# Attention and two feed-forward layers on one core: a transposed block is put in with the next pair's first blocks, and two weight chunks' low parts change engine

## The chip, the cores and the metric

The kernel runs on 1 core of one Trainium2 chip. The metric is the device time of one execution in microseconds (us). The engines are named as the profile names them: PE (TensorE; its weight loads are PEld), DVE (VectorE), ACT (ScalarE), POOL (GpSimd), SP (SyncE, which issues nearly all DMAs here). A difference below 0.2% (2 us) counts as no change.

## The reference

```python
# q, k, v: (4, 8, 576, 64), f: (4, 8, 576)
scores = matmul(q, k.T) / sqrt(64)
cum    = cumsum(log(clip(f, 1e-4, 1)))
scores = where(causal, -1e9, scores + cum[:, None] - cum[None, :])
attn   = softmax(scores)                    # over the keys
x = matmul(attn, v)                         # to (2304, 512)
h = x @ w_in0;  x = (h - tanh(h)) @ w_out0  # 512 -> 2048 -> 512
h = x @ w_in1;  x = (h * sigmoid(h)) @ w_out1
```

## The kernel before

Everything is float32. A product is made of three or four passes over high and low parts, so that PE does the most of the work. The program has two stages: the attention, which takes the first 178 us or so and in whose last part the first layer already begins, and the two feed-forward layers, which the change does not touch.

**The attention.** The 32 heads are worked off as 16 pairs p (`NP`). A pair has 576 queries: four blocks of 128 for each head and a last block of 64, and the last 64 queries of both heads share one tile of 128 rows. So a pair has nine tiles, grouped into four units u: unit 0 holds the query blocks 0 and 1 of both heads, unit 1 block 2, unit 2 block 3, and unit 3 the shared tile of the last queries. For each tile DVE adds the mask to the scores and takes the row's extreme (`least`, L462), ACT takes the exponential (`expo`, L470), POOL multiplies with one over the row's sum (`normalise`, L484). PE then transposes the tile block by block (`transposes`, L495) into the PSUM tiles `t`, each 2 KiB wide and four blocks of 128 columns long; ACT and DVE copy them to `ptf` in SBUF (`evac`, L535), and PE multiplies them with the values (`values`, L546). There are three buffers for the tiles `t` and two for the score tiles `s` (`scores`, L449 and, for the last queries, L441).

**The order of the work** is written out by hand under `manual_schedule`: a table `due` names for each of some 150 steps (a step is a tile; nine to a pair) what is called, and each engine runs its instructions in that order. The transposes of unit 3 of pair p come at the same place as the transposes of units 0, 1 and 2 of pair p+1 a few steps later (`steps_`, L620). Within a step the order is: transposes, values and scores on PE; then the copies (`evac`), the exponential, the extreme, the normalising, the loads and splits of a later pair (L385 on DVE, L383 and L391 on POOL), and last the decoding of weights.

**A round**, in what follows, is the time from PE's transposes of one pair's last queries (L495, source `pt`, five of them) to those of the next. On PE a round holds: unit 3 of pair p, unit 0 of pair p+1, the scores of unit 2 of pair p+2 (L449, 64x512), the transposes of unit 1, the scores of the last queries of pair p+2 (L441), the transposes of unit 2, the values of pair p, and the scores of units 0 and 1 of pair p+3. The scores of the last queries take the PSUM buffer of the scores of unit 1, so PE may begin them only when DVE has done `least` for both tiles of unit 1 (128x384 each).

**The fifth block.** The last queries have 576 keys, four and a half blocks of 128, so there are five transposes. Four go into one tile `t`, the fifth into column block 0 of a second one. That second tile is kept in `spare`; the next pair's unit 0 puts its two blocks of query block 0 ("the first blocks") into column blocks 1 and 2 of it. DVE copies the fifth block (128x128) and ACT the first blocks (128x256).

**Weights.** The two layers' weights come as 64-bit numbers and are decoded to a high and a low part, in 32 chunks of two matrices (m = 0, 1), each in seven stages (`wstages`, L143 on): `scale` (L153) and `split` (L163) on ACT; `shift` (L157), `exponent` (L167) and `low` (L170) on DVE; `rest` (L176) and `join` (L180) on POOL for chunks 0 to 4 and on DVE for the others. Chunks 0 and 1 are decoded during the attention, a stage every three to four steps (L657); chunks 2 to 4 at its end.

Of the kernel before, what the change touches and what calls it, by code (L numbers as in the profile page):

```python
# [7 lines left out]
F32 = mybir.dt.float32  # L8
# [6 lines left out]
P = 128  # L15
# [17 lines left out]
NEARLY, MID, LATE = 2, 3, 6  # L33
# [6 lines left out]
def forgetting_attention_two_ffn(  # L40
# [12 lines left out]
    nc = tc.nc  # L53
# [9 lines left out]
    def rd(ap):  # L63
        return ap.bitcast(F32)
# [78 lines left out]
    def wstages(k):  # L143

        l, c = chunks[k]
        slot = k % NSLOT
        tag = {m: f"{l}_{c}_{m}" for m in range(2)}
        a, b, w = {}, {}, {}
        eng = nc.gpsimd if k < NEARLY + MID else nc.vector

        def scale(m):
            high = rd(raws[k, m][:, :, 1])
            nc.scalar.activation(high, high, AF.Prelu, scale=2.0 ** -112, alpha=-(2.0 ** 32))  # L153

        def shift(m):
            a[m] = wtmp.tile([P, DM], U32, tag="wa", name=f"wa{tag[m]}")
            nc.vector.tensor_scalar(a[m], raws[k, m][:, :, 1], 3, None, ALU.logical_shift_left)  # L157

        def split(m):
            hi, lo = w[m] = [  # L160
                wpool[slot].tile([P, DM], F32R, tag=f"w{s}{slot}_{m}", name=f"w{s}{tag[m]}") for s in "hl"
            ]
            nc.scalar.copy(hi, rd(a[m]))  # L163

        def exponent(m):
            b[m] = wtmp.tile([P, DM], F32, tag="wb", name=f"wb{tag[m]}")
            nc.vector.tensor_scalar(b[m].bitcast(U32), a[m], 0xFF800000, None, ALU.bitwise_and)  # L167

        def low(m):
            nc.vector.scalar_tensor_tensor(  # L170
                b[m], raws.pop((k, m))[:, :, 0], 2.0 ** -52, b[m], ALU.mult, ALU.mult
            )

        def rest(m):
            hi, lo = w[m]
            eng.tensor_tensor(lo, rd(a[m]), rd(hi), ALU.subtract)  # L176

        def join(m):
            hi, lo = w[m]
            eng.tensor_tensor(lo, rd(lo), b[m], ALU.add)  # L180
            wtiles[l, c, m] = (hi, lo)

        return [(fn, m) for fn in (scale, shift, split, exponent, low, rest, join) for m in range(2)]
# [4 lines left out]
    def wdecode(k, left=0):  # L188


        if k not in stages:
            stages[k] = wstages(k)
        while len(stages[k]) > left:
            fn, m = stages[k].pop(0)
            fn(m)
            if not stages[k] and k > 1:
                wload(k + 2)
# [129 lines left out]
    def attention():  # L327
        with ExitStack() as actx:
# [4 lines left out]
            def pool(stack, name, bufs=1, **kw):  # L333
                return stack.enter_context(tc.tile_pool(name=name, bufs=bufs, side="right", **kw))
# [7 lines left out]
            ps_t = pool(actx, "ps_t", 3, space=PSUM)  # L342
# [4 lines left out]
            NP = B * NPAIR  # L347
# [5 lines left out]
            pt4 = [sp.tile([P, 640], F32, name=f"pt4_{i}", bufs=1) for i in range(2)]  # L353

            out_t = ps_r.tile([P, 512], F32, name="out_t")
            out_0, spare = {}, {}

            ptfs = [ptp.tile([P, 2, NPT], F32, name=f"ptf{i}") for i in range(2)]

# [63 lines left out]
            sps, ptile, rowsum, tps = {}, {}, {}, {}  # L423
# [62 lines left out]
            def transposes(p, u):  # L486

                ptf = ptfs[p % 2]
                rest = spare.pop("t", None) if u == 0 else spare.clear()
                tp = [ps_t.tile([P, 4, P], F32, tag="t", name=f"t{p}_{u}_{j}") for j in range(1 if rest else 2)]  # L490
                if rest:
                    tp.append(rest[:, 1:])

                def turn(j, k, pt, c):
                    nc.tensor.transpose(tp[j][:, k], pt[:, c * P:c * P + P], ident)  # L495

                def place(j, c0, nc_, i):
                    n = 2 * nc_
                    q = P * i + 448 * c0
                    dst = ptf[:, :, q:q + 448 * nc_] if nc_ > 1 else ptf[:, :, q:q + P]  # L500
                    src = tp[j][:, 0:n]
                    if nc_ > 1:
                        dst = dst.rearrange("p h (c w) -> p h c w", w=448)[:, :, :, 0:P]
                        src = src.rearrange("p (h c) w -> p h c w", h=2)
                    return src, dst

                if u == 3:
                    ptile.pop((p, 2, 4))
                    pt = pt4[p % 2]
                    spare["t"] = tp[1]  # L510
                    for c in range(5):
                        turn(c // 4, c % 4, pt, c)
                    dst = ptf[:, :, 512:512 + 4 * 448].rearrange("p h (c w) -> p c h w", w=448)[:, :, :, 0:64]
                    o = 448 * 4 + 512
                    tps[p, u] = [
                        (tp[0].rearrange("p c (h w) -> p c h w", h=2), dst),
                        (tp[1][:, 0].rearrange("p (h w) -> p h w", h=2), ptf[:, :, o:o + 64]),
                    ]
                    return
                pts = {t: ptile.pop((p,) + t)[0] for t in units[u]}  # L520
                i = u + 1
                if u == 0:
                    for h in range(2):
                        turn(1, h, pts[h, 0], 0)
                for j in range(2 if u else 1):
                    for h in range(2):
                        for k in range(min(2, i + 1 - 2 * j)):
                            turn(j, min(2, i + 1 - 2 * j) * h + k, pts[h, i], 2 * j + k)
                tps[p, u] = [place(j, 2 * j, min(2, i + 1 - 2 * j), i) for j in range(2 if u else 1)]
                if u == 0:  # L530
                    tps[p, u].append(place(1, 0, 1, 0))

            def evac(p, u):
                for j, (src, dst) in enumerate(tps.pop((p, u))):
                    (nc.vector.tensor_copy if j == (u > 0) else nc.scalar.copy)(dst, src)  # L535

            def values(p, part):

# [83 lines left out]
            for p in range(NP):  # L622
                n0 = NTILE * p
                for u, k in enumerate((-1, 0, 4, 6)):
                    if p + u:
                        later(n0 + k, scores, p, u)
                k = ends_.get(p, steps_)
                for u in range(4):
                    later(n0 + k[u], transposes, p, u)
                    later(n0 + k[u] + 1, evac, p, u)  # L630
                later(n0 + k[4], values, p, [(0, 0), (64, 0), (64, 1), (64, 2), (64, 3), (64, 4)])
                later(n0 + k[4] + 1, collect, p, 0, 64)
                later(n0 + k[4] + 1, collect, p, 64, S)
# [35 lines left out]
            for n in range(N + 2 * NTILE):  # L669
                if n % NTILE == 0:  # L670
                    run(n, scores)
                    run(n, transposes)
                    run(n, values)
                else:
                    run(n, transposes)
                    run(n, values)
                    run(n, scores)
                if n < NTILE - 1:
                    busy(kqs[0][:, 0], 2)
                run(n, evac)  # L680
                if has(n - 1):
                    expo(n - 1)
                run(n, collect)
                if n % 3 == 2 and has(n - 5):
                    guard(n - 5)
                if has(n):
                    least(tiles[n])
                if n % 3 == 2 and has(n - 5):
                    normalise(n - 5)
                run(n, load_kq, load_v, split, place_last, place_dec, place_dec_last)  # L690
                for fn, *a in ahead.get(n - N, []):
                    fn(*a)
# [4 lines left out]
    with tc.manual_schedule():  # L697
        attention()
        for n in range(len(steps) + HL):
            if n > HL:  # L700
                front(n)
            if n >= HL:
                project(n - HL)
# [39 lines left out]
```

## Time and profile before

| what | value |
|---|---|
| median of 3 runs | 984.08 us (983.68 to 984.15) |
| the profiled execution's own time | 984.0 us |
| its span, first to last instruction | 982.1 us |
| PE busy | 964.6 us, 98% of the span |
| DVE, ACT, POOL busy | 555.8, 454.8, 183.6 us |
| granted clock of PE | 1.0 throughout |

How to read it: a share of busy time is a mean over the whole program. POOL works only in the first 210 us and is busy there nearly all the time; DVE and ACT are busy some seven tenths of the attention. In a timeline a row gives the start, the duration, engine, line, operation, the tiles written and read, the shape, how many instructions are put together, and in brackets the idle time ahead of the first of them with what ended it. Matmuls overlap, so the duration of several is less than their sum.

### The profile page before, as it was taken

How to read it: one execution, taken by the hardware profiler on the slowest of the kernel's cores; microseconds unless marked ns; L12 is line 12 of the kernel's file. 1: busy time of each engine (PE TensorE's matmuls, PEld its weight loads, DVE VectorE, ACT ScalarE, POOL GpSimd, SP SyncE). 2: the span in 40 equal slices, each digit the busy share in tenths (PEclk: the TensorE clock that was granted, in tenths of full speed). 3: DMA queues.
4: the chain of work that ended last, by engine and by line, in shares of the span. 5: the costliest groups of instructions: out<-in, count | busy, mean ns of one | idle time of the engine just before them, and what ended most of it. 6: DMA issues, size and time to landing. Idle time of an engine off the chain costs nothing.

```text
span 982.1 us, 13857 instructions
## 1 busy us (share of the span) xinstructions
PE 964.6 (98%) x5208; PEld 791.5 (81%) x5208; DVE 555.8 (57%) x1221; ACT 454.8 (46%) x979; POOL 183.6 (19%) x266
## 2 busy tenths in 40 slices
PE   8999999999999999999999999999999999999998
PEld 6766666778988889888889888888888888888887
DVE  7667676686865456664668653354444544633323
ACT  6777777744543424343434443343444433433222
POOL 8979989740000000000000000000000000000000
PEclk9999999999999999999999999999999999999999
DMA  4433222421211011100112110111111000001111
GB/s 154 147 120 136 87 92 83 149 100 43 86 44 43 1 43 65 65 21 23 43 43 87 43 43 1 44 43 43 43 43 43 36 24 29 1 1 43 44 43 65
DMA packets 21699, 56.67 MB, mean 58 GB/s; under 512 B 6848, under 2 KB 6848, under 8 KB 21600
## 3 DMA queue, kind: packets, MB, share of 16 engines
q1 hardware_dynamic: 21624, 55.77, 16.1%
q8 instruction: 41, 0.67, 0.3%
q14 instruction: 26, 0.21, 0.1%
q10 hardware_dynamic: 8, 0.02, 0.0%
HBM read 49.35 MB, written 5.31 MB: 56 GB/s over the span
## 4 chain that ended last, share of the span: by engine, by line
PE 94%; DVE 3%; POOL 1%; issue 1%; DMA 0%; ACT 0%; SPq 0%; POOLq 0%; DVEq 0%
PE a L314 40%; PE h L255 39%; PE s L449 4%; PE out_t L546 4%; PE t L495 3%; PE s L441 2%; DVE p L462 1%; PE out_t L574 1%; POOL wl L180 1%; POOL wl L176 0%; DVE ptf L535 0%; PE out L546 0%; DMA kqraw<-kq 0%; DVE kqs L385 0%; POOL gl L277 0%
## 5 line engine op out<-in xcount | busy, mean ns | idle before, releaser
L255 PE MATMUL h<-xh,wl 128*128 128x512 f32 (+1 forms) x640 | 235.7, 368 | 2.2 <-POOL wl L180 2.2
L255 PE MATMUL h<-xh,wh 128*128 128x512 f32 (+1 forms) x640 | 236.0, 369 | 0.0
L255 PE MATMUL h<-xl,wh 128*128 128x512 f32 (+1 forms) x640 | 235.6, 368 | 0.0
L277 DVE TENSOR_TENSOR gl<-g,gh 128x512 fp32r<-128x512 f32 (+1 forms) x158 | 101.4, 642 | 99.9 <-ACT gh L273 98.0
L255 PEld LDWEIGHTS h<-xh,wl 128*128 128x128 f32 x640 | 120.6, 188 | 23.1 <-POOL wl L180 3.0
L255 PEld LDWEIGHTS h<-xh,wh 128*128 128x128 f32 x640 | 120.7, 189 | 20.6
L255 PEld LDWEIGHTS h<-xl,wh 128*128 128x128 f32 x640 | 120.6, 188 | 20.4
L273 ACT CAST gh<-g 128x512 fp32r<-128x512 f32 (+1 forms) x160 | 92.6, 579 | 95.8 <-DVE g L270 93.3
L314 PE MATMUL a<-gl,wh 128*128 128x512 f32 (+1 forms) x320 | 117.8, 368 | 0.0
L314 PE MATMUL a<-gh,wh 128*128 128x512 f32 (+1 forms) x320 | 117.7, 368 | 0.0
L314 PE MATMUL a<-gh,wl 128*128 128x512 f32 (+1 forms) x320 | 117.7, 368 | 0.0
L314 PE MATMUL a<-wh,gh 128*128 128x512 f32 x288 | 112.2, 390 | 0.0
L314 PE MATMUL a<-wl,gh 128*128 128x512 f32 x288 | 112.2, 390 | 0.0
L314 PE MATMUL a<-wh,gl 128*128 128x512 f32 x288 | 112.0, 389 | 0.0
L272 ACT ACTIVATE g<-h 128x512 f32<-128x512 f32 (+1 forms) x80 | 44.3, 554 | 113.6 <-PE h L255 96.3
L243 DVE TENSOR_TENSOR xl<-y,xh 128x512 fp32r<-128x512 f32 (+1 forms) x60 | 37.4, 638 | 96.6 <-ACT xh L241 96.6
L462 DVE CUSTOM_DVE_ANT_0 p<-s,mask 128x128 f32<-128x128 f32 (+3 forms) x128 | 59.9, 478 | 43.8 <-PE s L449 37.0
L241 ACT CAST xh<-y 128x512 fp32r<-128x512 f32 (+1 forms) x60 | 34.2, 580 | 104.8 <-PE h L255 103.1
L470 ACT ACTIVATE p<-p,mn 128x128 f32<-128x128 f32 (+3 forms) x128 | 71.1, 558 | 8.5 <-DVE mn L462 6.0
L484 POOL TENSOR_SCALAR p<-p,sm 128x128 f32<-128x128 f32 (+3 forms) x128 | 67.7, 548 | 18.3 <-DVE sm L481 18.3
L243 DVE TENSOR_TENSOR xl<-x,xh 128x512 fp32r<-128x512 f32 (+1 forms) x56 | 34.2, 632 | 61.6 <-ACT xh L241 61.6
L314 PEld LDWEIGHTS a<-gl,wh 128*128 128x128 f32 x320 | 60.3, 189 | 10.1
(92 smaller groups left out, 1388.9 us busy)
## 6 DMA issues: line engine op xcount, KB each, us to landing
raw<-w_in SPq DMA_DIRECT2D x32, 512.0 KB
raw<-w_out SPq DMA_DIRECT2D x32, 512.0 KB
kqraw<-kq SPq DMA_DIRECT2D x16, 608.0 KB
vraw<-v SPq DMA_DIRECT2D x16, 320.0 KB
out<-ob SPq DMA_DIRECT2D x18, 256.0 KB
lq<-kqs SPq DMA_DIRECT2D x32, 32.0 KB
dec<-x SPq DMA_DIRECT2D x1, 576.0 KB
de<-dec SPq DMA_DIRECT2D x28, 17.0 KB
```

The source lines that it names most:

```text
L241: nc.scalar.copy(hi[:, :n], src[:, k, t0:t0 + n])
L243: eng.tensor_tensor(lo[:, :n], src[:, k, t0:t0 + n], rd(hi[:, :n]), ALU.subtract)
L255: nc.tensor.matmul(hp[:, :n], w[:, k * P:k * P + P], m[:, :n], start=(k == 0 and r == 0), stop=(k == NKT - 1 and r == 2),)
L272: nc.scalar.activation(g[:, :n], hp[:, :n], AF.Silu)
L273: nc.scalar.copy(gh[:, :n], g[:, :n])
L277: eng.tensor_tensor(gl[:, :n], g[:, :n], rd(gh[:, :n]), ALU.subtract)
L314: nc.tensor.matmul(dst, w, m, start=(first and r == 0), stop=(last and r == 2))
L449: nc.tensor.matmul(s[:, h, c:c + n], a[half(h), q], b[half(h), 0:n], start=r == 0, stop=r == 3,)
L462: nc.vector.tensor_tensor_reduce(out=pt.rearrange("p (g c) -> p g c", g=2) if i == 4 else pt, in0=src, in1=m, op0=ALU.add, op1=ALU.min, sc ...
L470: nc.scalar.activation(pt, pt, AF.Exp, bias=mn, scale=-1.0, accum_out=sums[:, n // 3 % 5, n % 3, 0:1],)
L484: nc.gpsimd.tensor_scalar(pt, pt, sm[:, j:j + 1], 1.0, ALU.mult, ALU.mult)
L546: nc.tensor.matmul(dst, vraw[p][:, h, D * c:D * c + D], ptfs[p % 2][:, h, 448 * c + a:448 * c + q1], start=c == 0, stop=c == last,)
```

## The change

It touches two things. **The fifth block:** for pairs 0 to 13 the unit 3 has only four transposes and one tile `t` (`alone`). The fifth transpose is done at the beginning of the next pair's unit 0 (`fifth(p - 1, 1, 2)`), into column block 2 of that unit's own second tile, whose blocks 0 and 1 hold the first blocks; there is no `spare` any more. Its copy is still made by DVE, behind the copies of the first and second query blocks, and the engine of a copy is now chosen by `j % 2`. **The low parts:** `rest` and `join` of chunks 0 and 1 are given to DVE in place of POOL, 8 instructions of 128x512 in all.

```diff
-        eng = nc.gpsimd if k < NEARLY + MID else nc.vector
+        eng = nc.gpsimd if NEARLY <= k < NEARLY + MID else nc.vector
...
-            out_0, spare = {}, {}
+            out_0 = {}
...
             def transposes(p, u):
 
                 ptf = ptfs[p % 2]
-                rest = spare.pop("t", None) if u == 0 else spare.clear()
-                tp = [ps_t.tile([P, 4, P], F32, tag="t", name=f"t{p}_{u}_{j}") for j in range(1 if rest else 2)]
-                if rest:
-                    tp.append(rest[:, 1:])
+                alone = u == 3 and p < NP - 2
+                tp = [ps_t.tile([P, 4, P], F32, tag="t", name=f"t{p}_{u}_{j}") for j in range(1 if alone else 2)]
...
+                def fifth(p, j, k):
+                    turn(j, k, pt4[p % 2], 4)
+                    o = 448 * 4 + 512
+                    return tp[j][:, k].rearrange("p (h w) -> p h w", h=2), ptfs[p % 2][:, :, o:o + 64]
+
                 if u == 3:
                     ptile.pop((p, 2, 4))
-                    pt = pt4[p % 2]
-                    spare["t"] = tp[1]
-                    for c in range(5):
-                        turn(c // 4, c % 4, pt, c)
+                    for c in range(4):
+                        turn(0, c, pt4[p % 2], c)
                     dst = ptf[:, :, 512:512 + 4 * 448].rearrange("p h (c w) -> p c h w", w=448)[:, :, :, 0:64]
-                    o = 448 * 4 + 512
-                    tps[p, u] = [
-                        (tp[0].rearrange("p c (h w) -> p c h w", h=2), dst),
-                        (tp[1][:, 0].rearrange("p (h w) -> p h w", h=2), ptf[:, :, o:o + 64]),
-                    ]
+                    tps[p, u] = [(tp[0].rearrange("p c (h w) -> p c h w", h=2), dst)]
+                    if not alone:
+                        tps[p, u].append(fifth(p, 1, 0))
                     return
                 pts = {t: ptile.pop((p,) + t)[0] for t in units[u]}
                 i = u + 1
+                last = [fifth(p - 1, 1, 2)] if u == 0 < p < NP - 1 else []
...
                 if u == 0:
-                    tps[p, u].append(place(1, 0, 1, 0))
+                    tps[p, u] += [place(1, 0, 1, 0)] + last
 
             def evac(p, u):
                 for j, (src, dst) in enumerate(tps.pop((p, u))):
-                    (nc.vector.tensor_copy if j == (u > 0) else nc.scalar.copy)(dst, src)
+                    (nc.vector.tensor_copy if j % 2 == (u > 0) else nc.scalar.copy)(dst, src)
```

The order on PE in the round that goes from pair 6 to pair 7, before. `t_3_0` and `t_3_1` are the two tiles of unit 3 of pair 6, `pt` its last queries' tile, `p_0` and `t_0_0` belong to unit 0 of pair 7; in brackets stand the engines whose semaphores an instruction waits for (the engine, not which of its instructions).

```order
L495 MATMUL t_3_0_1492<-ident,pt_0_106 128x128 x3
L495 MATMUL t_3_1_1493<-ident,pt_0_106 128x128 [waits DVE_49]
L495 MATMUL t_3_1_1493<-ident,p_0_1284 128x128 [waits DVE_49,Pool_49]
L495 MATMUL t_3_1_1493<-ident,p_0_1284 128x128 [waits Pool_49]
L495 MATMUL t_0_0_1534<-ident,p_0_1284 128x128 [waits Activation_49,Pool_49]
...
L449 MATMUL s_2_1541<-kqs_1340 128x512 [waits DVE_49]
```

The same place of the change:

```order
L493 MATMUL t_3_0_1492<-ident,pt_0_106 128x128 x3
L493 MATMUL t_0_1_1532<-ident,pt_0_106 128x128 [waits DVE_49]
L493 MATMUL t_0_1_1532<-ident,p_0_1284 128x128 [waits Pool_49] x2
L493 MATMUL t_0_0_1531<-ident,p_0_1284 128x128 [waits Activation_49,Pool_49]
...
L449 MATMUL s_2_1540<-kqs_1338 128x512 [waits DVE_49]
```

The fifth transpose now shares a tile that was not in use, and the first blocks behind it wait for POOL alone; their wait for DVE is gone.

The order on DVE at that place, before: the piece from `least` of unit 0's first tile (L462, two rows each) to `least` of unit 1's second tile (`mn_1_2`), without the rows of the tiles in between.

```order
L385 TENSOR_REDUCE kqs_1508<-kqraw_1343 128x640 [waits DMAHW7_49,DMAHW6_49,DMAHW5_49]
L535 COPY ptf_109<-t_3_1_1493 128x2x64 [waits PE_49]
L462 ISA p_0_1452,mn_1_0_1517<-s_0_1451,mask 128x128
...
L462 ISA p_1_1483,mn_0_2_1552<-s_1_1482,mask 128x384 [waits Pool_49]
L535 COPY ptf_110<-t_0_0_1534 128x2x2x128 [waits PE_49]
L477 TENSOR_REDUCE sm_1559<-sums 128x3 [waits Activation_49]
L462 ISA p_1_1483,mn_1_2_1561<-s_1_1482,mask 128x384
```

And of the change:

```order
L385 TENSOR_REDUCE kqs_1506<-kqraw_1341 128x640 [waits DMAHW7_49,DMAHW6_49,DMAHW5_49]
L176 TENSOR_TENSOR wl_0_0_1139<-wa_0_0_1004,wh_0_0_1138 128x512
L462 ISA p_0_1452,mn_1_0_1514<-s_0_1451,mask 128x128
...
L462 ISA p_1_1483,mn_0_2_1551<-s_1_1482,mask 128x384 [waits PE_49,Pool_49]
L176 TENSOR_TENSOR wl_0_1_1188<-wa_0_1_1043,wh_0_1_1187 128x512
L535 COPY ptf_110<-t_0_0_1531 128x2x2x128 [waits PE_49]
L535 COPY ptf_109<-t_0_1_1532 128x2x64 [waits Activation_49]
L477 TENSOR_REDUCE sm_1559<-sums 128x3
L462 ISA p_1_1483,mn_1_2_1561<-s_1_1482,mask 128x384
```

The copy of the fifth block has gone from behind L385 to behind the copy of `t_0_0`, ahead of `least` of unit 1's second tile, and where it waited for PE it now waits for ACT; the count that it waits for in the built program is the one that ACT's copy of the first blocks out of the same tile sets. It is so in all 14 rounds. The two `rest` of chunk 0 stand here. Of the eight moved instructions six stand ahead of a fifth copy in this way: both `rest` of chunk 0 in this round, both `join` of chunk 1 in the round that begins at 158.10 us in the trace of before, and one each in the rounds that begin at 103.97 and 147.40 us; the other two stand behind it. On ACT the order of the instructions is as before.

## Rows read from the trace of the kernel before

**Rows 1.** The page's head: span, and busy time of each engine.

```profile
span 982.1 us, 13857 instructions
PE 964.6 (98%) x5208; PEld 791.5 (81%) x5208; DVE 555.8 (57%) x1221; ACT 454.8 (46%) x979; POOL 183.6 (19%) x266
```

**Rows 2.** Timeline of PE: starts of rounds, and one round's first half.

```profile
38.55 0.77 PE L495 MATMUL t<-ident,pt 128*128 128x128 f32 x5
...
49.26 0.76 PE L495 MATMUL t<-ident,pt 128*128 128x128 f32 x5
...
158.10 0.77 PE L495 MATMUL t<-ident,pt 128*128 128x128 f32 x5
159.34 0.85 PE L495 MATMUL t<-ident,p 128*128 128x128 f32 x6 [0.47 <-DVE ptf L535]
...
162.03 0.64 PE L441 MATMUL s<-kqs,lq 128*128 128x288 f32 x3
...
168.80 0.77 PE L495 MATMUL t<-ident,pt 128*128 128x128 f32 x5
```

**Rows 3.** Who waited for whom, 0 to 212 us: total us, times, longest.

```profile
PEld s L449 <- DVE mn L462: 6.3, 16, 0.9
PE t L495 <- DVE ptf L535: 6.2, 13, 0.5
```

**Rows 4.** Timeline of DVE in the round from 158.10 us.

```profile
158.91 0.29 DVE L535 COPY ptf<-t 128x128 f32<-128x128 f32 x1 [0.25 <-PE t L495]
159.11 0.28 DVE L462 CUSTOM_DVE_ANT_0 p<-s,mask 128x128 f32<-128x128 f32 x1
...
160.62 0.69 DVE L535 COPY ptf<-t 128x512 f32<-128x512 f32 x1
161.22 0.15 DVE L477 TENSOR_REDUCE sm<-sums 128x3 f32<-128x6 f32 x1
161.28 0.55 DVE L462 CUSTOM_DVE_ANT_0 p<-s,mask 128x384 f32<-128x384 f32 x1
161.76 0.09 DVE L462 DVE_READ_ACCUMULATOR2_ANT mn<- 128x1 f32 x1
```

**Rows 5.** Timeline of ACT in that round: two of its copies.

```profile
158.80 0.58 ACT L535 COPY ptf<-t 128x512 f32<-128x512 f32 x1 [1.81 <-PE t L495]
...
161.04 0.36 ACT L535 COPY ptf<-t 128x256 f32<-128x256 f32 x1
```

**Rows 6.** Timeline of ACT: that copy in the rounds from 49.26 and 125.61 us.

```profile
52.76 0.36 ACT L535 COPY ptf<-t 128x256 f32<-128x256 f32 x1
...
129.58 0.36 ACT L535 COPY ptf<-t 128x256 f32<-128x256 f32 x1
```

**Rows 7.** Timeline of PE: last queries' scores in four other rounds, and two starts.

```profile
53.20 0.64 PE L441 MATMUL s<-kqs,lq 128*128 128x288 f32 x3
...
59.98 0.77 PE L495 MATMUL t<-ident,pt 128*128 128x128 f32 x5
...
64.45 0.66 PE L441 MATMUL s<-kqs,lq 128*128 128x288 f32 x3
...
114.67 0.76 PE L495 MATMUL t<-ident,pt 128*128 128x128 f32 x5
...
118.80 0.67 PE L441 MATMUL s<-kqs,lq 128*128 128x288 f32 x3
...
129.55 0.64 PE L441 MATMUL s<-kqs,lq 128*128 128x288 f32 x3
```

**Rows 8.** Timeline of DVE: the end of `least` that the scores at 118.80 awaited.

```profile
118.66 0.08 DVE L462 DVE_READ_ACCUMULATOR2_ANT mn<- 128x1 f32 x1
```

**Rows 9.** DVE's groups by line; timelines of DVE and POOL: two-input instructions of 128x512.

```profile
L176 DVE TENSOR_TENSOR wl<-wa,wh 128x512 fp32r<-128x512 f32 x54 | 35.4, 683 | 0.0
...
140.43 1.29 DVE L170 SCALAR_TENSOR_TENSOR wb<-raw,wb 128x512 f32<-128x512 uint32 x1
...
159.71 1.28 POOL L180 TENSOR_TENSOR wl<-wl,wb 128x512 fp32r<-128x512 f32 x1
```

## The prediction

> **What bounds the kernel now.** I read the page's head first, then the waits of the attention, then the timelines of PE, DVE and ACT through one round. The head says that PE is busy for 98% of the span [rows 1]; so only what PE waits for can be won, and what delays PE is lost. The layers behind the attention are not touched: whatever PE gains or loses in the 14 rounds shifts them as a whole. In the attention the largest wait of PE itself is for DVE's copy out of a tile `t`, 6.2 us in 13 times [rows 3]. A round lasts 10.71 us (38.55 to 49.26) and 10.70 (158.10 to 168.80) [rows 2]. In the latter one sees the wait: five transposes, then 0.47 us in which PE stands still for the 128x128 copy [rows 2], which DVE does at 158.91 after idling 0.25 us for PE [rows 4]. The first blocks go into the same tile, at other columns, and wait until DVE has read the fifth.
>
> Three chains meet in a round. PE's own is one. DVE's goes over the five `least` of units 0 and 1 that PE needs before the scores of the last queries at 162.03 [rows 2]; the last of them ends at 161.76 + 0.09 = 161.85 [rows 4]. Behind the weight loads PE already waits for an earlier `least` as well, 6.3 us in 16 times [rows 3]. ACT's begins with its copy at 158.80, and four exponentials lie between that and its copy of the first blocks at 161.04, which ends at 161.40 [rows 5].
>
> **What is removed.** The wait of PE, 0.47 us a round [rows 2]. On DVE the idle 0.25 us and the copy, 0.20 from its start to the next [rows 4], go from the front of the chain: DVE comes 0.45 us sooner to everything up to the copy of 160.62, behind which it arrives at 161.22 - 0.45 = 160.77 us of this round [rows 4].
>
> **What takes its place.** There the fifth copy now stands, and it waits for ACT's copy of the first blocks out of its tile. That copy does not come sooner: it hangs on ACT's own chain, which begins when PE has done the first four transposes, as before. So DVE stands still from 160.77 to 161.40 + 0.06 (hand-over, as from a `least` that ended at 118.66 + 0.08 [rows 8] to the scores at 118.80 [rows 7]) = 161.46: 0.69 us. Queued behind it on DVE are the row sums (L477) and `least` of unit 1's second tile, and PE's scores of the last queries wait for that one. Step by step: 161.46, + 0.20 for the copy, + 0.06 for L477, + 0.48 to the reading of the extreme [rows 4], + 0.08 for the reading [rows 8], + 0.06 hand-over = 162.34. The scores begin there in place of 162.03 [rows 2]: **+0.31 us** in a plain round, that is 0.94 us behind the end of ACT's copy. What PE does behind them is unchanged, and the copies there wait for PE. What PE gains at the front of the round it stands still for ahead of these scores.
>
> **The rounds that are not plain.** The rule is the same: the scores come 0.94 us behind the end of the first blocks' copy.
> - In the round from 49.26 one weight decode step of ACT is queued ahead of that copy, which ends at 52.76 + 0.36 = 53.12 [rows 6]; 54.06 in place of 53.20 [rows 7] is +0.86. The round from 71.25 is like it: together +1.72. Before, ACT's delay cost PE next to nothing there.
> - In the round from 125.61 two such steps stand there: 129.58 + 0.36 + 0.94 = 130.88 [rows 6] for 129.55 [rows 7], +1.33. The round from 168.80 has two casts of `x` at that place: together +2.66.
> - In four rounds DVE's own decode steps delayed the scores before. They now fall into DVE's wait. A plain round's scores will come 162.34 - 158.10 = 4.24 us after its start. The round from 59.98 gives 64.22 for 64.45, -0.23; the one from 114.67 gives 118.91 for 118.80, +0.11 [rows 7]; the two others lie between. Together about 0.
> - Six plain rounds (from 27.74, 38.55, 93.27, 103.97, 147.40 and 158.10): 6 x 0.31 = +1.86.
>
> **The low parts.** POOL loses 8 instructions of 1.28 us [rows 9]. They are off the path: the round from 158.10 has two of them and lasts 10.70, the one from 38.55 has none and lasts 10.71 [rows 2]. So their going is worth nothing. DVE gets 8 of 0.68, the price of the same line for later chunks, when POOL is idle [rows 9]. With POOL at work beside it I bound it by 0.68 below and by the 1.29 of the two-input L170 at 140.43 above [rows 9], and take 0.68, because at those places POOL mostly waits or runs one-input instructions. Six stand ahead of a fifth copy. Where one stands alone, 0.68 fits into the wait of 0.69: nothing. Where two do (rounds from 93.27 and 158.10), 2 x 0.68 - 0.69 = 0.67 is left, together **+1.34**. The two behind the copy delay only copies that have time.
>
> **The sum:** 1.86 + 1.72 + 2.66 + 0 + 1.34 = +7.6 us. Against the profiled execution's 984.0 that is 991.6; the median of 984.08 is the same within 0.1 us, so I forecast 991.6.
>
> **A rule against the trace.** The row of PE's 0.47 us shows a writer kept from a tile while DVE reads other columns of it [rows 2]; no row shows two readers of one tile. The Trainium skill, PSUM — Partial Sum Buffer, section "PSUM bank collisions raise a hardware error", says that no two engines may be in the same bank and the same 32 partitions at once, reads against reads included, and that semaphores have to guard the bank and not the address. By that rule the fifth copy has to come after ACT's, as in the sum above, +7.6; if only writers had to be kept from readers, it would be the first rival below. The trace agrees for a writer and a reader (0.47 us); for two readers no run here shows it yet.
>
> **The rivals.**
> - *The wait costs nothing, and the change does what its first half looks like.* The point from which this decides: ACT's copy would have to be done by 160.77, 0.63 us sooner than it ends now. Then `least` ends 0.45 sooner and 0.20 later, 161.60, and the scores start at 161.66 for 162.03: -0.37 a round, 14 x 0.37 = 5.2, **978.8**. For it: the wait of 6.2 us is real [rows 3]. Against it: ACT has no gap between 158.80 and 161.04 that could close, and the awaited count is that copy's. Chance 0.07.
> - *Gain and loss cancel.* As the first rival, but with DVE then the bound of every round, so that the six moved instructions lengthen it by 0.68 each: 5.2 - 4.1 = 1.1 gained, **982.9**; or the lateness of ACT's copy is half made up by slack that I don't see. Chance 0.07.
> - *DVE and POOL hinder each other more.* At 1.29 us each, the two rounds with a pair of moved instructions lose 2 x 1.29 - 0.69 = 1.89 and the two with one lose 0.60: 4.98 in place of 1.34, **995.2**. For it: the 1.29 at 140.43 [rows 9]; against it: by then DVE and POOL need not meet, because DVE's early part lies where POOL waits for row sums. Chance 0.13.
> - The forecast: chance 0.73.
>
> **How the numbers follow.** The third rival is the high end, 995.2. The low end is the forecast with the moved instructions at nothing and the four rounds of late ACT at a plain round's price: 10 x 0.31 = 3.1, 987.1. Range 987.0 to 995.2; beyond it lie the two rivals on the other side, 0.14, and a little of the third. About 0.2% (2 us) is what a measurement tells from no change: faster 0.07, same 0.07, slower 0.86.
>
> **What the profile after would show.** Right: the wait of PE's transposes for DVE's copy is gone; in its place DVE waits 14 times for ACT's copy (L535), 0.6 to 0.7 us in a plain round and over 1 us in those from 125.61 and 168.80; the wait of the last queries' scores (L441) for `least` grows to some 10 us; plain rounds last 11.0 us, and the longest are those with two ACT steps or two moved instructions. ACT's wait for the extremes grows too. Wrong: if plain rounds last 10.4 us, the ACT copy is not what DVE waits for; if they last 11.0 and the sum still differs, the moved instructions' or ACT's steps are mis-sized, and the rounds tell which.

## The result and the profile after

| | before | after |
|---|---|---|
| median | 983.6 us (6 runs, 983.42 to 984.15) | 991.4 us (6 runs, 990.56 to 992.67) |
| the profiled execution | 984.0 us | 990.82 us |
| its span | 982.1 us | 988.9 us |

The ratio is 1.0079 (95% interval 1.0066 to 1.0092): the change makes the kernel 7.8 us slower by the medians and 6.8 us by the two profiled executions. The two differ because in three of the six runs of the changed kernel PE's mean granted clock is 0.997 or 0.998 (991.99 to 992.67 us) and in the other three 0.999 or 1.0 (990.56 to 990.82); the profiled one is of these, and what the clock does is told at the end.

The head of the page of the changed kernel, for [rows 1]:

```profile
span 988.9 us, 13857 instructions
PE 965.5 (98%) x5208; PEld 792.2 (80%) x5208; DVE 560.6 (57%) x1229; ACT 455.9 (46%) x979; POOL 175.9 (18%) x258
```

PE does the same work, 965.5 for 964.6 us; the span grew by what it waits. Eight instructions went from POOL to DVE. Who waited for whom in the changed kernel, from 0 to 212 us (total us, times, longest), for [rows 3]:

```profile
PEld s L441 <- DVE mn L462: 12.3, 15, 2.1
PE s L441 <- DVE mn L462: 8.5, 12, 1.9
DVE ptf L535 <- ACT ptf L535: 8.0, 8, 2.2
...
PEld t L493 <- DVE ptf L535: 0.2, 1, 0.2
```

The 6.2 us that PE's transposes waited for DVE's copy are gone (0.2 of its weight loads is left). In their place stands a wait that the kernel before did not have, DVE's copy (L535) for ACT's copy, and PE's scores of the last queries (L441) wait 8.5 us for the extremes behind it.

A plain round of the changed kernel, from 38.94 us, on PE, for [rows 2]:

```profile
38.94 0.77 PE L493 MATMUL t<-ident,pt 128*128 128x128 f32 x5
...
43.15 0.67 PE L441 MATMUL s<-kqs,lq 128*128 128x288 f32 x3 [0.59 <-DVE mn L462]
...
49.97 0.77 PE L493 MATMUL t<-ident,pt 128*128 128x128 f32 x5
```

The same round on DVE, for [rows 4], and on ACT, for [rows 5]:

```profile
40.90 0.69 DVE L535 COPY ptf<-t 128x512 f32<-128x512 f32 x1
42.27 0.29 DVE L535 COPY ptf<-t 128x128 f32<-128x128 f32 x1 [0.68 <-ACT ptf L535]
42.47 0.15 DVE L477 TENSOR_REDUCE sm<-sums 128x3 f32<-128x6 f32 x1
42.54 0.55 DVE L462 CUSTOM_DVE_ANT_0 p<-s,mask 128x384 f32<-128x384 f32 x1
43.01 0.08 DVE L462 DVE_READ_ACCUMULATOR2_ANT mn<- 128x1 f32 x1
```

```profile
41.88 0.35 ACT L535 COPY ptf<-t 128x256 f32<-128x256 f32 x1
```

Read from below: the scores begin at 43.15 because the extreme is read out at 43.01 + 0.08; that one stands behind the row sums and the fifth copy, which starts at 42.27; and that copy waited 0.68 us for ACT's copy out of the same tile, which ends at 41.88 + 0.35 = 42.23. The round lasts 49.97 - 38.94 = 11.03 us, where it lasted 10.71 before.

In the round with two ACT decode steps the same wait is longer. DVE, ACT and PE there:

```profile
133.13 0.29 DVE L535 COPY ptf<-t 128x128 f32<-128x128 f32 x1 [1.71 <-ACT ptf L535]
```

```profile
130.34 0.61 ACT L163 CAST wh<-wa 128x512 fp32r<-128x512 f32 x1
...
132.23 0.60 ACT L163 CAST wh<-wa 128x512 fp32r<-128x512 f32 x1
132.74 0.36 ACT L535 COPY ptf<-t 128x256 f32<-128x256 f32 x1
```

```profile
134.01 0.66 PE L441 MATMUL s<-kqs,lq 128*128 128x288 f32 x3 [1.62 <-DVE mn L462]
```

All 14 rounds, from the starts of PE's transposes (L495 before, L493 after), in us. "Scores" is the time from the start of the round to the first scores of the last queries.

| round before | length | scores | length after | scores | what stands in it |
|---|---|---|---|---|---|
| 27.74 | 10.81 | 4.03 | 11.02 | 4.21 | |
| 38.55 | 10.71 | 3.93 | 11.03 | 4.21 | |
| 49.26 | 10.72 | 3.94 | 11.58 | 4.78 | one ACT step |
| 59.98 | 11.27 | 4.47 | 11.01 | 4.20 | DVE steps |
| 71.25 | 10.81 | 3.92 | 11.53 | 4.73 | one ACT step |
| 82.06 | 11.21 | 4.40 | 11.20 | 4.38 | DVE steps |
| 93.27 | 10.70 | 3.92 | 11.44 | 4.64 | two low parts ahead |
| 103.97 | 10.70 | 3.92 | 11.02 | 4.21 | one low part ahead |
| 114.67 | 10.94 | 4.13 | 11.02 | 4.21 | DVE step |
| 125.61 | 10.74 | 3.94 | 12.04 | 5.24 | two ACT steps |
| 136.35 | 11.05 | 4.26 | 11.02 | 4.21 | DVE step |
| 147.40 | 10.70 | 3.93 | 11.03 | 4.21 | one low part ahead |
| 158.10 | 10.70 | 3.93 | 11.45 | 4.65 | two low parts ahead |
| 168.80 | 8.93 | 3.93 | 10.23 | 5.24 | two casts of `x` on ACT |

The last round ends at 177.73 before and at 184.54 after. That is 6.81 us: 6.63 in the rounds and 0.18 ahead of the first, which says little, since in the twelve profiles of all kernels here the first round begins anywhere from 27.39 to 27.92. Behind the last round nothing more is lost: the profiled executions differ by 6.82.

### The profile page after: what moved, and what is told of

The parts are those of the page before. It is cut to its first block, busy times and chain, and to the rows that moved or that the text cites. A ratio compares the mean times of both kernels' runs of the same rounds, so it can differ in the third digit from the quotient of the medians.

```text
span 988.9 us, 13857 instructions
## 1 busy us (share of the span) xinstructions
PE 965.5 (98%) x5208; PEld 792.2 (80%) x5208; DVE 560.6 (57%) x1229; ACT 455.9 (46%) x979; POOL 175.9 (18%) x258
## 4 chain that ended last, share of the span: by engine, by line
PE 87%; DVE 4%; POOL 3%; issue 2%; ACT 2%; DMA 1%; SPq 1%; POOLq 0%; DVEq 0%; ACTq 0%
PE a L314 39%; PE h L255 39%; PE out_t L546 3%; PE t L493 2%; PE s L449 2%; PE s L441 2%; DVE p L462 1%; ACT p L470 1%; DVE kqs L385 1%; POOL p L484 1%; DMA dec<-x 1%; DVE ptf L535 1%; POOL wl L176 0%; POOL kqs L391 0%; PE out L546 0%
## 5 line engine op out<-in xcount | busy, mean ns | idle before, releaser
L462 DVE CUSTOM_DVE_ANT_0 p<-s,mask 128x128 f32<-128x128 f32 (+3 forms) x128 | 60.0, 479 | 41.3 <-PE s L449 32.5
L484 POOL TENSOR_SCALAR p<-p,sm 128x128 f32<-128x128 f32 (+3 forms) x128 | 69.5, 561 | 32.7 <-DVE sm L481 13.8
L314 PEld LDWEIGHTS a<-gh,wl 128*128 128x128 f32 x320 | 60.3, 188 | 10.1
```

Source lines behind the costliest of these rows:

```text
L314: nc.tensor.matmul(dst, w, m, start=(first and r == 0), stop=(last and r == 2))
L462: nc.vector.tensor_tensor_reduce(out=pt.rearrange("p (g c) -> p g c", g=2) if i == 4 else pt, in0=src, in1=m, op0=ALU.add, op1=ALU.min, sc ...
L484: nc.gpsimd.tensor_scalar(pt, pt, sm[:, j:j + 1], 1.0, ALU.mult, ALU.mult)
```

## The experiments

Theory A is the prediction's: DVE waits for ACT's copy out of the same tile, and the extreme that PE needs is queued behind that wait. Theory B is that the place ahead of the extreme, or the extra DVE work, costs the time, whoever waits for whom. The lengths of rounds come from each run's own trace.

### 1. The fifth block alone

```diff
-        eng = nc.gpsimd if NEARLY <= k < NEARLY + MID else nc.vector
+        eng = nc.gpsimd if k < NEARLY + MID else nc.vector
```

> The moved fifth block alone; the low parts of chunks 0 and 1 are back on POOL. Theory A (the loss is DVE's wait for ACT's copy out of the same tile, with the extremes of unit 1 queued behind it): nearly all of the loss stays. Plain rounds 11.02 us as in the changed kernel; only the rounds with two moved instructions (11.44 and 11.45) fall to 11.02, 0.85 together, so 990.0 to 990.7. Theory B (the moved instructions are what DVE cannot carry, 8 x 0.68 or more): 984 to 987, plain rounds 10.7 us.

Measured: 991.08 us (989.58 to 991.32), ratio 1.0072 (1.0058 to 1.0086). The two rounds of 11.44 and 11.45 us now take 11.02 and 11.01; the plain rounds stay at 11.01 to 11.03, and those with two ACT steps at 12.07 and 10.24. The median is 0.4 above the expected band, the profiled execution (989.58) 0.4 below it. So nearly all of the loss is the fifth block's; in the rounds the low parts add 0.85 us.

### 2. The low parts alone

The kernel before with the line of experiment 1 the other way round.

> The low parts alone on DVE; the fifth block as in the kernel before. Theory A: there is no wait on DVE that covers them now, only 0.25 us of idle time ahead of the fifth copy and about 0.1 us ahead of the last queries' scores. Two rounds get two of them in the part of DVE's chain that PE waits for (0.43 + 0.6 each), two rounds get one (0.55 each), four are behind it: about 3.1 us lost, 986.5 to 987.2. So the parts do not add up to the whole: 6.9 and 3.1 for 7.8. Theory C (they lay on POOL's path and relieve it there): 982 to 984.

Measured: 986.33 us (986.16 to 986.67), ratio 1.0027 (1.0017 to 1.0037), a little under the band. (Of the eight instructions two, not four, stand behind the part that PE waits for.) The two rounds with two low parts take 11.47 and 11.44 us (10.70 before), those with one 11.30 and 11.32. In the first of them PE's wait for the fifth copy has grown:

```profile
94.28 0.85 PE L495 MATMUL t<-ident,p 128*128 128x128 f32 x6 [0.73 <-DVE ptf L535]
```

The parts do not add up: 7.55 (991.08 - 983.53) and 2.80 (986.33 - 983.53) against 7.8 for both. In the changed kernel the low parts lie in DVE's wait; without that wait they cost more.

### 3. The fifth copy first

Everything as in the changed kernel; only the order of the copies in `evac` differs, so that DVE's fifth copy comes ahead of its 128x512 copy, and ACT's copy has to wait for it.

```diff
-                for j, (src, dst) in enumerate(tps.pop((p, u))):
+                jobs = list(enumerate(tps.pop((p, u))))
+                for j, (src, dst) in jobs[2:] + jobs[:2]:
```

> The changed kernel with one thing exchanged: DVE copies the fifth block ahead of the 128x512 copy of the step and, in program order, ahead of ACT's copy of the first blocks; so ACT would wait for DVE, at a time when DVE has long been done. Same instructions, same number on each engine. Theory A: DVE's wait goes, PE's 0.47 us stays saved; a plain round takes 10.33 us, and the six moved instructions in DVE's chain cost 0.6 to 0.68 each, as nothing covers them: 982 to 984. Theory B (a place ahead of the extremes costs the round, whoever waits for whom): 990 to 992.

Measured: 983.1 us (982.9 to 983.34), ratio 0.9994 (0.9986 to 1.0003): 8.3 us less than the changed kernel by an exchange of two copies, and no difference to the kernel before. A plain round on DVE, then ACT's copy in it, then PE:

```profile
39.62 0.88 DVE L536 COPY ptf<-t 128x128 f32<-128x128 f32 x2
40.42 0.14 DVE L477 TENSOR_REDUCE sm<-sums 128x3 f32<-128x6 f32 x1
```

```profile
40.59 0.36 ACT L536 COPY ptf<-t 128x256 f32<-128x256 f32 x1
```

```profile
37.65 0.77 PE L493 MATMUL t<-ident,pt 128*128 128x128 f32 x5
...
41.10 0.66 PE L441 MATMUL s<-kqs,lq 128*128 128x288 f32 x3
...
47.89 0.77 PE L493 MATMUL t<-ident,pt 128*128 128x128 f32 x5
```

DVE makes both copies in one go, ACT comes to the tile when DVE has left it, and the round takes 10.24 us in place of 11.03. Theory B falls: the copy stands ahead of the extreme as before. The rounds with two low parts, nothing covering them any more, take 11.46 us both.

### 4. The fifth copy first, low parts on POOL

Both edits above.

> As the run before it, with the low parts back on POOL. Theory A: 14 rounds of 10.33 us where no decode step of DVE stands in them, 978 to 980, faster than both kernels. Theory B: 990 to 991. A third outcome, about 983.5 with plain rounds of 10.7, would say that something else (POOL's or ACT's chain) sets a round at 10.7 as soon as PE's wait is gone.

Measured: 981.08 us (980.22 to 982.08), ratio 0.9972 (0.9962 to 0.9983): faster than both kernels, but 1 to 2 us short of what I expected. Five rounds take 10.25 to 10.29 us, the last one 9.13, the other eight 10.47 to 11.18. In the round from 69.45 one sees one reason: DVE, having lost one wait for ACT, meets the next.

```profile
71.42 0.89 DVE L536 COPY ptf<-t 128x128 f32<-128x128 f32 x2
72.55 0.16 DVE L477 TENSOR_REDUCE sm<-sums 128x3 f32<-128x6 f32 x1 [0.25 <-ACT p L470]
```

The row sums wait for ACT's exponentials, which an ACT decode step has delayed, and the extreme stands behind them. This holds for two of the eight long rounds (69.45 and 123.12). In four others DVE's own decode steps make the scores late (58.53, 80.27, 112.31, 133.87), and in two the scores are in time and PE's weight loads then wait for POOL's normalising (L484), 0.37 us in the round from 101.70 and 0.2 in that from 154.71. The price of plain rounds was right; I had taken too many rounds for plain.

### 5. The fifth copy behind the extreme

`evac` puts the fifth copy aside, and it is done right behind `least` of the same step; low parts on POOL.

```diff
+                late.extend(jobs[2:])
+                for j, (src, dst) in jobs[:2]:
...
                     least(tiles[n])
+                while late:
+                    _, (src, dst) = late.pop()
+                    nc.vector.tensor_copy(dst, src)
```

> Low parts on POOL. DVE copies the fifth block behind the extreme of unit 1's second tile (one instruction pair later than in the changed kernel), and behind ACT's copy of the first blocks, for which it still waits. Theory A (the wait costs only what is queued behind it and awaited by PE): nothing that PE needs soon stands behind it now, so plain rounds take 10.25 us as with the fifth copy first, and the rounds in which DVE's chain is late (10.6 to 11.2 there) gain up to the 0.20 us of the copy: 979.5 to 981.5. Theory D (two readers of one tile cost their length wherever the copy stands): plain rounds of 10.5 us or more, 984 or more.

Measured: 980.52 us (980.01 to 981.47), ratio 0.9968 (0.9957 to 0.998). Plain rounds take 10.16 or 10.17 us, 0.09 less than with the copy first. DVE in one of them (the fifth copy is L692), then ACT's copy:

```profile
40.67 0.08 DVE L462 DVE_READ_ACCUMULATOR2_ANT mn<- 128x1 f32 x1
40.87 0.29 DVE L692 COPY ptf<-t 128x128 f32<-128x128 f32 x1
```

```profile
40.49 0.35 ACT L537 COPY ptf<-t 128x256 f32<-128x256 f32 x1
```

The copy still follows ACT's, but in a plain round hardly any wait is left: 0.12 us, from 40.75 to 40.87. Theory D falls, since such a round takes 10.16 us and not 10.5. The profile lists three rounds in which DVE does wait, 2.0 us in all. The extremes ahead of the copy are not held up by it: in the rounds from 47.71 and 122.37 the scores come 3.41 and 3.79 us after the start, against 3.45 and 3.79 in experiment 4. But the rounds take 10.53 and 10.98 us, 0.24 and 0.23 more than in experiment 4, because DVE's copy that PE's transposes of unit 2 await is queued behind the wait. DVE and PE in the second of them:

```profile
126.74 0.29 DVE L692 COPY ptf<-t 128x128 f32<-128x128 f32 x1 [0.64 <-ACT ptf L537]
```

```profile
128.09 0.66 PE L493 MATMUL t<-ident,p 128*128 128x128 f32 x4 [0.17 <-DVE ptf L537]
```

So a wait of 0.64 us cost 0.23 us with that queue behind it. In the changed kernel a wait of 0.68 us in a plain round, with the extreme behind it, goes with a round 0.86 us longer than here (11.02 for 10.16).

### 6. The row sums behind the extreme

On top of experiment 4.

```diff
-                if n % 3 == 2 and has(n - 5):
-                    guard(n - 5)
                 if has(n):
                     least(tiles[n])
+                if n % 3 == 2 and has(n - 5):
+                    guard(n - 5)
```

> Low parts on POOL, fifth block copied first (the kernel that measured 981.1), and in each step the row sums (L477) behind the extreme in place of ahead of it. Theory A: with the wait for ACT's copy gone, the next thing that DVE waits for there is ACT's exponential ahead of the row sums (0.25 us in the rounds with ACT decode steps). With the extreme ahead of it, those rounds (10.82, 10.75, 10.58 us) lose 0.2 to 0.4 each: 979.5 to 980.5. Theory E (these rounds are long by POOL or by DVE's own decode steps): no change, 981.

Measured: 982.16 us (981.4 to 983.18), ratio 0.9984 (0.9975 to 0.9993): 1.1 us slower than experiment 4, where I expected about 1 us less. The scores do come 3.53 and 3.51 us after the start in the two rounds with ACT steps (3.78 and 3.79 before the edit), but in the plain ones they come at 3.50 to 3.52 too (3.45 before), and these now take 10.30 to 10.32. The rounds with ACT steps stay at 10.95 and 10.74, since PE then waits behind the scores: in the first for DVE's copy out of a tile `t`, as below, in the second 0.37 us for ACT's copy.

```profile
75.08 0.66 PE L493 MATMUL t<-ident,p 128*128 128x128 f32 x4 [0.41 <-DVE ptf L536]
```

DVE in a plain round of this kernel, then in that of experiment 4:

```profile
38.80 0.15 DVE L477 TENSOR_REDUCE sm<-sums 128x3 f32<-128x6 f32 x1
38.99 0.18 DVE L481 RECIPROCAL sm<-sm 128x3 f32<-128x3 f32 x1
```

```profile
38.66 0.15 DVE L477 TENSOR_REDUCE sm<-sums 128x3 f32<-128x6 f32 x1
38.73 0.41 DVE L462 CUSTOM_DVE_ANT_0 p<-s,mask 128x256 f32<-128x256 f32 x1
```

The reciprocal, now right behind the row sum that it reads, starts 0.19 us after it; an independent instruction started after 0.07. My edit put two instructions next to each other of which one reads the other's result, so the extremes behind them come later in every round.

### 7. The decode steps where DVE and ACT idle

On top of experiment 4: the stages of chunks 0 and 1 at the end of a pair's last tile.

```diff
-                at((40, 87)[k // NSTAGE] + 46 * (k % NSTAGE) // NSTAGE - N,
+                at((44, 89)[k // NSTAGE] + (0, 0, 9, 9, 18, 18, 18, 18, 27, 27, 28, 32, 35, 38)[k % NSTAGE] - N,
```

> Low parts on POOL, fifth block copied first, and the decode stages of ACT and DVE for chunks 0 and 1 put where both engines idle: at the end of a pair's last tile, ahead of the next pair's first extremes (DVE idles 2.6 to 3.4 us there, ACT 1.8). Theory A: what keeps 8 of 14 rounds at 10.5 to 11.2 us is decode steps ahead of the extremes; all rounds fall towards 10.25 to 10.35, some 4 us in all: 976.5 to 978.5. Theory E (POOL's chain sets these rounds, or the price of the steps only moves): 980 to 982.

Measured: 978.3 us (977.99 to 979.1), ratio 0.9946 (0.9934 to 0.9959). Eleven rounds take 10.24 to 10.26 us, the last one 8.93. Two take 11.16 and 11.12: there POOL has become late. PE in the first of them:

```profile
104.64 0.44 PE L493 MATMUL t<-ident,p 128*128 128x128 f32 x2 [0.26 <-POOL p L484]
105.31 0.87 PE L493 MATMUL t<-ident,p 128*128 128x128 f32 x6 [0.23 <-POOL p L484]
```

They are the two rounds in which PE had waited for POOL in experiment 4 already. The six others that were long there take 10.24 to 10.26 us now, so it was decode steps of DVE and ACT that kept them long.

### 8. Both

> The two edits of the runs before it together. If the row sums' wait is late only through ACT's decode steps, the second edit adds nothing to the first: the same as with the decode stages alone, within 0.5 us. If DVE waits for ACT there in every round, 1 us less or more than that.

Measured: 978.88 us (978.59 to 979.49), ratio 0.9952 (0.994 to 0.9965), 0.6 us more than experiment 7. Plain rounds take 10.31 us again: the second edit does harm and no good, as in experiment 6.

### 9. The low parts on DVE, in the gap

On top of experiment 7, the low parts on DVE again, at the steps `..., 27, 27, 27, 36, 36, 36`.

> As the kernel with the decode stages in the gap (978.3), and the low parts of chunks 0 and 1 on DVE again, in that gap too: three of the 128x512 steps at the end of a pair's last tile in two pairs for each chunk. It tells the place of the moved instructions from their engine. Theory A: on DVE they cost what stands between them and the extremes, and in the gap that is nothing (idle 2.6 to 3.4 us against 3 x 0.7 to 0.9); and the two rounds of 11.16 and 11.12 us, in which PE waits for POOL behind its low parts, fall to 10.3: 976 to 977. Theory F (DVE pays for them anywhere): 980 to 983.

Measured: 976.44 us (976.03 to 977.2), ratio 0.9925 (0.9913 to 0.9938). Twelve of the first thirteen rounds take 10.24 to 10.26 us, one of the two late ones among them; the other takes 10.58 in place of 11.16. In it PE waits 0.53 us for an extreme (L449), where it waits 0.21 in a plain round: DVE begins L385 0.23 us late, and the profile shows no wait for that, so the reason stays open. Over the 14 rounds the same eight instructions on DVE add 0.85 us in the change, add 2.6 in experiment 2, where no wait covers them, and take 1.5 off here. The last figure is against experiment 7, where POOL's low parts made two rounds late by 0.9 us each; POOL with them at other steps was not tried in that kernel.

### 10. The fifth copy behind the extreme, with that

> As the run before it, but with the fifth block copied behind the extreme of unit 1's second tile in place of ahead of ACT's copy. Theory A: rounds of 10.16 to 10.2 in place of 10.25, 14 x 0.08 = 1.1 us less: 975 to 976. If the copy's wait for ACT holds up the extremes behind it, no gain against the run before it.

Measured: 975.76 us (975.33 to 976.03), ratio 0.9918 (0.9904 to 0.9931), 8.0 us less than the kernel before. Twelve rounds take 10.16 to 10.19 us. The gain over experiment 9 is 0.7 us, where 14 x 0.08 had been expected: the first 13 rounds gain 1.00 us, and the last loses 0.25 (9.17 for 8.92), the one round in which DVE still waits for ACT's copy (0.64 us). So both halves of the change can pay, if the copy stands behind the extreme and the low parts stand in DVE's idle time. But the 8 us are not theirs alone: by the medians 3.1 came with the late copy in experiment 5, and 2.8 lie between experiments 4 and 7, which differ only in the place of the decode stages, and that is no part of the change.

## Why the prediction was right

**The wait that goes** went, as the waits show. **The wait that comes** is 0.68 us in the row, for a predicted 0.69, but that they meet is luck: the row counts from the end of the copy ahead of it, and my 0.69 from the time when DVE would start the next instruction. Counted like that the wait is 42.27 - 40.90 - 0.60 = 0.77. What bounds the round is ACT's copy, so the price hardly depends on it. From the end of ACT's copy to the scores it was 43.15 - 42.23 = 0.92 us for 0.94, so the scores came 4.21 us after the round's start for a predicted 4.24, and a plain round grew by 0.32 or 0.33 for a predicted 0.31 (only the first by 0.21). Experiments 3 and 5 show the cause from two sides: with the copy ahead of ACT's there is no wait, with the copy behind the extreme there is one of 0.12 us at most, and in both a plain round takes 10.2 us.

**The rounds with late ACT** follow the same rule: 4.78 us to the scores in the round from 49.97 (predicted 54.06 - 49.26 = 4.80), 5.24 in that from 128.77 (130.88 - 125.61 = 5.27). The four give 0.86 + 0.72 + 1.30 + 1.30 = 4.18 us for a predicted 4.38. **The four rounds with DVE steps** give -0.26 - 0.01 + 0.08 - 0.03 = -0.22 for a predicted 0.

**The low parts** were mis-sized: +1.34 predicted, 0.87 measured (rounds 95.29 and 162.86 in experiment 1 against the changed kernel; 0.85 over all 14). The failing step is "2 x 0.68 - 0.69". DVE in that round:

```profile
95.02 0.81 DVE L385 TENSOR_REDUCE kqs<-kqraw 128x640 fp32r<-128x640 f32 x1
95.75 0.68 DVE L176 TENSOR_TENSOR wl<-wa,wh 128x512 fp32r<-128x512 f32 x1
96.35 0.28 DVE L462 CUSTOM_DVE_ANT_0 p<-s,mask 128x128 f32<-128x128 f32 x1
...
97.85 0.69 DVE L176 TENSOR_TENSOR wl<-wa,wh 128x512 fp32r<-128x512 f32 x1
98.47 0.88 DVE L535 COPY ptf<-t 128x512 f32<-128x512 f32 x2
```

The duration is 0.68, but the next instruction starts after 0.60 and 0.62: a queued instruction delays the next by its pitch, the time from its start to the next one's start. With the pitch, and with the wait of 0.77 as the cover, 0.60 + 0.62 - 0.77 = 0.45 is left a round; 0.43 was measured in each. For the copies I had used start to start, and for these not. The cover was short by the same slip: the idle 0.25 us that goes from the front of DVE's chain counts from the end of L385's duration, and the next instruction can start 0.08 us before that end (the first two rows above: 95.02 + 0.81 = 95.83, and 95.75).

**The rival of a dearer DVE** had its price and not its place: two of the eight took 1.18 and 1.38 us (156.58 and 101.42 us), but these are the two behind the copy, where DVE has time; the other six took 0.66 to 0.69. Beside these two POOL ran its two-input L391, and beside the six it waited or ran the one-input L484, as I had assumed. L391 alone does not explain them: in experiment 2 the same two took 0.77 and 0.71 us beside it. **The rival in which the wait costs nothing** is what experiments 4 and 5 make true; they measured 981.1 and 980.5 where it said 978.8, because not all rounds were plain. Its price for a plain round was too low by the slip above: 0.46 saved with the copy first (10.71 to 10.25) for a predicted 0.37.

**Wrong in a detail:** I said that DVE would wait 14 times for ACT's copy. The trace shows 8, from 0.28 to 2.22 us; in the other six rounds DVE's own steps fill the time, as my sum had it and my list of signs had not. Behind the round with two ACT steps (12.04) the longest are those with one (11.58 and 11.53), and not those with two low parts (11.45). And ACT's wait for the extremes did not grow (6.0 us before, 5.3 after); its wait for DVE's reciprocal (L481) did, from 1.2 to 5.7. The sum was 0.8 us too high for the profiled execution (991.6 for 990.82): 0.5 by the low parts and 0.2 each by the rounds with late ACT and those with DVE steps, less the 0.18 ahead of the first round. That it lies 0.2 from the median is luck: three of the six runs are longer, at a lower clock, and the sum did not hold that.

**Two readers of one tile:** DVE does wait for ACT's copy of other columns of its tile, 0.28 to 2.22 us, so the program keeps readers apart too. The Trainium skill, PSUM — Partial Sum Buffer, section "PSUM bank collisions raise a hardware error", asks for that: semaphores have to guard the bank and not the address. The trace agrees as far as the program goes; what the chip would do if both read at once was not tried.

## What to carry to other kernels

When a copy is moved next to another reader of the same tile, ask who gets to the tile first, and what stands in the waiting engine's queue behind it: the same two copies in the other order, or one instruction pair later, made 8 to 11 us of difference here. What is queued behind a wait sets its price. A wait that PE no longer has is worth only what the next wait leaves of it, so list the second wait of each round as well. And price a queued instruction from its start to the next one's start, in the place where it will stand: the same eight instructions added 0.85 us to the rounds, added 2.6, and took 1.5 off, by what stood around them and what the other engine was spared.

## What was not expected of the hardware

PE's clock falls in some executions of the same kernel and not in others. At the end of the attention PE waits nearly 2 us for POOL's low parts of a later chunk (L180). Below are that wait and the stretches behind it in experiment 8 (windows: busy time of each engine, then granted clock, DMA share, GB/s), and the same wait in experiment 7:

```profile
195.40 0.50 PE L255 MATMUL h<-xh,wl 128*128 128x512 f32 x1 [1.83 <-POOL wl L180]
```

```profile
196.00:197.00 1.00, 1.00 (x4) 0.81 (x3) 1.00 (x2) 0.00 (x0) 1.00 (x2) 0.57 0.00 0
197.00:198.00 1.00, 1.00 (x4) 0.72 (x3) 1.00 (x2) 0.00 (x0) 1.00 (x1) 0.50 0.00 0
198.00:199.00 1.00, 1.00 (x4) 0.81 (x3) 1.00 (x2) 0.00 (x0) 1.00 (x2) 0.50 0.00 0
199.00:200.00 1.00, 1.00 (x4) 0.79 (x4) 1.00 (x1) 0.00 (x0) 1.00 (x2) 0.72 0.30 53
200.00:201.00 1.00, 1.00 (x6) 0.79 (x5) 1.00 (x2) 0.00 (x0) 1.00 (x1) 1.00 0.85 287
```

```profile
194.97 0.50 PE L255 MATMUL h<-xh,wl 128*128 128x512 f32 x1 [1.82 <-POOL wl L180]
```

```profile
196.00:197.00 1.00, 1.00 (x6) 0.82 (x5) 1.00 (x2) 0.00 (x0) 1.00 (x2) 1.00 0.00 0
197.00:198.00 1.00, 1.00 (x6) 0.83 (x5) 1.00 (x1) 0.00 (x0) 1.00 (x2) 1.00 0.00 0
```

In the one the granted clock falls to 0.50, the lower of the two levels (1.2 GHz), for (0.43 + 0.50 + 0.50 + 0.28) / 0.50 = 3.4 us, so PE is set back by 1.7 us of work; in the other it stays at 1.0 after the same wait. The profiled execution of experiment 5 shows a fall too (0.50 from 198 to 201 us, after a wait of 1.80), those of the kernels before and after do not (waits of 1.66 and 1.69). The kernel loses less than 1.7 us: from the end of that wait to the end of the span it is 781.3 to 781.4 us in the ten profiles without a fall, and 782.2 in the two with one, 0.8 us more. In those two PE's next wait for POOL, 0.51 us in experiment 7, is gone, which makes up a part. The runs of experiment 5 fit: 980.01 to 980.16 us at a mean clock of 1.0, and 980.88 to 981.47 at 0.998. The runs of the changed kernel lie further apart than one such fall, 990.56 to 990.82 and 991.99 to 992.67; no profile was taken of one of the longer ones, so what happened in them is not shown.
